# The second angle table of a one-core SSM and gated-mix kernel: nine direct slots times w and two chained complex products in place of eight slots and four products

## The chip, the cores and the metric

The kernel runs on one core of a Trainium2 chip. The metric is the device time of one execution in microseconds. The kernel before takes 200.22 us (median of three runs, 199.91 to 201.16). A measured execution is a little longer than the span of its profile, which runs from the first to the last instruction that was recorded.

Five engines work side by side, each through its own queue in order: PE (matrix products), DVE (element-wise work on vectors), ACT (functions, scaling, copies out of PSUM), POOL (fills) and SP (which here only issues transfers). They wait for each other through semaphores.

## The reference, cut to what matters

```
x = u                                    # (1, 2048, 512), bf16
g = sigmoid((x * gate_w).sum(-1))
# a: a long convolution over the 2048 positions, for each of 512 channels d
dt    = exp(log_dt)                                   # (512, 1)
logdA = dt * (A_re + 1j*A_im)                         # (512, 128)
P     = exp(logdA[:, :, None] * l)                    # l = arange(2048), rounded to bf16
K     = einsum("dn,dnl,dn->dl", C, P, dt * B).real    # (512, 2048)
a     = irfft(rfft(u, padded) * rfft(K, padded)) + u * Dskip
# b: the two positions with the largest x @ w_r go through a gated FFN, and are added to x
b     = x + scatter(y_selected * sigmoid(r_selected))
out   = g * a + (1 - g) * b
```

The lag l is rounded to bf16, so above 256 only every second, fourth or eighth lag is distinct. Every distinct lag is the sum of a first part t1 (multiples of 8, up to 248, 32 of them) and a second part t2 (21 of them, in the list T2). So the kernel needs exp(logdA * t1) and w * exp(logdA * t2) as two tables per channel, with w = C * dt * B, and forms K for all pairs by matrix products over the 128 states n.

## The kernel before, in words

Channels go in two halves h = 0, 1 of 256. The states n lie on the 128 partitions. The work of a half is this chain:

- `exps1`, `exps2` (L533, L536) on ACT: real exponentials (magnitudes) of the table slots, one ACTIVATE of 128x512 for each slot, for both halves at once. Those of `exps2` for half 1 go to `ST` and are parked in DRAM (`park`, L880), since their place in SBUF is needed in between. L897 brings them back into `EB[1]` and `BS[1]`.
- `trig` (L541): for four angles at a time, four scaled angles (`SCL`, L404, on ACT or DVE), a sine (ACT), a scalar step on DVE that adds a quarter turn (L554), and the second sine, which is the cosine. The angle and sine buffers (`ARG`, `SNC`) are two, used in turn.
- `tab1(h)` (L559): the first table, 32 values of t1, products of magnitudes with sines and cosines on DVE.
- `tab2(h)` (L585): the second table `TQ[h]`, 21 slots, imaginary and real part. Slots 0 to 7 (t2 = 0..7) are made directly and multiplied by w. Eight factors for steps of 256 are made in `BS`. Slots 8 to 20 are four complex products (`far`, L609) of earlier slots with such factors. A complex product (`cmul`, L569) is six DVE operations: four products into scratch `QA` and two sums.
- `kgen(h)` (L748): 128 table products on PE (L756), copied out into `KA[h]`; then the selection matmuls (L769, L772, L775), which pick and regroup the columns of `KA` into `KC`. Its slots are grouped by four in the order of T2.
- `kspec(h)` (L779): the spectrum of K by matmuls with constants `KP` (L791), loaded at L896 over the place of the first table of half 0, so once `kgen(0)` is done.
- `products(h)` (L797): spectrum of u times spectrum of K on DVE, most of it in operations of 128x2048.
- `inverse(h)` (L830): inverse transform on PE (L845), scaled by the gate, added, and written out.

Beside it run `routing` (gate, selection of two positions and the FFN), `forward` (the transform of u in two blocks, L736 and L738: a group is eight matmuls, in the second block with a ninth) and `xupd` (L868, the update of x on PE, L873 and L874, and ACT).

Buffers share places. `TQ[1]` lies over `KA[0]`, so `tab2(1)` may write only after the selection of half 0 has read it; its real part also lies over `NG`, constants of `forward`. `EB[1]` lies over `TQ[0]`, so the parked magnitudes come back after the table products of half 0.

Nobody writes the order of the engines' queues by hand. `Prog.op` (L67) collects operations with the buffers and keys that they read and write; `Prog.schedule` (L107) puts them into one queue per engine, by a planned start, and among equal ones by the longest planned path to the end plus a priority (`boost`, `prio`). Operations of the helpers `EV` (copies out of PSUM, L400) and `SCL` go to ACT or DVE, whichever the plan has free earlier. So an edit of one function moves instructions on all engines. The helpers' lines in the profile are L387 (`TT`, product or sum of two tensors on DVE), L391/L392 (`TS`, scalar step on DVE), L394 (`STT`), L398 (`AC`, ACT), L402 (`EV`), L406 (`SCL`) and L409 (a transfer). A DVE operation that reads or writes a key of an earlier DVE operation waits for that one's semaphore.

## Time and profile before

| | us |
|---|---|
| median of three runs | 200.22 |
| the profiled execution | 200.09 |
| its span | 198.3 |
| DVE busy in the span | 170.9 (86%), 281 instructions |
| PE busy | 162.3 (82%), 1490 matmuls |
| ACT busy | 140.8 (71%), 232 instructions |
| POOL busy | 3.4 (2%) |
| mean granted PE clock | 0.944 of full speed |

Times in the profile count from the start of the span. A timeline row has the start, the length, engine, line, operation, the shapes of output and input, and how many instructions were merged; in brackets, how long the engine was idle ahead of it and what ended that. A row of a window has the length of the window and for each engine the busy time and number of instructions, then the granted PE clock, the busy share of the transfer engines and GB/s. A row of a group has the busy time, the mean length of one in ns, and the idle time ahead. [...]

### The profile page before, as it was taken

Reading aid. Unit: us, or ns where it says so; the run is one execution under the profiler, and the core shown is the slowest. Engines: PE = TensorE matmul, PEld = TensorE weight load, DVE = VectorE, ACT = ScalarE, POOL = GpSimd, SP = SyncE. Lnnn points to the kernel's source line nnn. Section 1 sums busy time; section 2 is a strip of 40 time slices with the busy share of each in tenths; the row PEclk is TensorE's granted clock in tenths of the full one; section 3 lists DMA queues with packets and bytes.
Section 4 is the critical chain, followed back from the end, with each engine's and each line's share of the span. In section 5 each row is a group of like instructions: output and inputs, shape, how many; then the busy total and the mean of one; then the engine's idle time right before and its main releaser. Section 6 shows DMA issues by size and latency. Waiting matters only on the chain.

```text
span 198.3 us, 3623 instructions
## 1 busy us (share of the span) xinstructions
PE 162.3 (82%) x1490; PEld 106.5 (54%) x1490; DVE 170.9 (86%) x281; ACT 140.8 (71%) x232; POOL 3.4 (2%) x7
## 2 busy tenths in 40 slices
PE   0074599999999999999996499950988999999791
PEld 0063434774344444455753038740866888888680
DVE  0659635599999999999768999999999999999983
ACT  3669999979999999879999984640663553642500
POOL 6000000000000000000000000000000000000000
PEclk9999759999999999999999759996699999999998
DMA  5999999309320220200089400000029000012333
GB/s 92 281 259 370 293 410 406 95 8 338 82 53 3 53 53 0 53 3 0 3 304 451 198 2 3 0 0 0 3 46 377 3 0 3 0 46 71 98 106 106
DMA packets 22097, 23.17 MB, mean 117 GB/s; under 512 B 13121, under 2 KB 19394, under 8 KB 21442
## 3 DMA queue, kind: packets, MB, share of 16 engines
q1 hardware_dynamic: 20738, 22.63, 35.5%
q10 hardware_dynamic: 1344, 0.33, 1.4%
q8 instruction: 11, 0.18, 0.3%
q14 instruction: 4, 0.03, 0.0%
HBM read 19.02 MB, written 3.15 MB: 112 GB/s over the span
## 4 chain that ended last, share of the span: by engine, by line
PE 61%; DVE 19%; ACT 11%; DMA 4%; SPq 1%; issue 1%; DVEq 0%
PE ps L736 29%; DVE AR L387 17%; PE ps L791 7%; ACT AR L398 5%; ACT AR L402 5%; PE ps L845 5%; PE ps L756 5%; DMA AR<-in_A_u_dram 4%; PE ps L769 3%; PE ps L738 2%; PE ps L873 2%; PE ps L711 2%; DVE AR L394 2%; PE ps L625 1%; PE ps L874 1%; PE ps L700 1%
## 5 line engine op out<-in xcount | busy, mean ns | idle before, releaser
L387 DVE TENSOR_TENSOR AR<-AR 128x1024 bf16<-128x1024 bf16 (+7 forms) x184 | 135.4, 796 | 7.8 <-DMA AR<-in_A_A_re_dram 6.3
L402 ACT ACTIVATE AR<-ps 128x1024 bf16<-128x1024 f32 (+4 forms) x56 | 44.0, 810 | 27.8 <-PE ps L791 14.0
L398 ACT ACTIVATE AR<-AR 128x512 bf16<-128x512 f32 (+4 forms) x84 | 59.5, 773 | 5.2 <-DVE AR L391 2.5
L736 PE MATMUL ps<-AR 128*128 128x512 bf16 x256 | 61.3, 391 | 0.0
L736 PEld LDWEIGHTS ps<-AR 128*128 128x128 bf16 x256 | 25.3, 100 | 30.7 <-issue 3.4
L845 PE MATMUL ps<-AR 128*128 128x256 bf16 x256 | 28.7, 273 | 1.1 <-DVE AR L387 1.1
L398 ACT ACTIVATE AR<-ps,AR 128x256 bf16<-128x256 f32 (+1 forms) x40 | 20.3, 564 | 10.1 <-PE ps L845 5.4
L791 PE MATMUL ps<-AR 128*128 128x256 bf16 x224 | 26.0, 274 | 1.7 <-ACT AR L402 1.7
L845 PEld LDWEIGHTS ps<-AR 128*128 128x128 bf16 x256 | 24.9, 98 | 4.5 <-DVE AR L387 1.6
L791 PEld LDWEIGHTS ps<-AR 128*128 128x128 bf16 x224 | 21.7, 99 | 6.1 <-ACT AR L402 3.1
L406 ACT ACTIVATE AR<-AR 128x256 int32<-128x256 f32 (+1 forms) x50 | 21.1, 483 | 0.1
L756 PE MATMUL ps<-AR 128*128 128x84 bf16 x256 | 13.4, 213 | 8.0 <-DVE AR L387 7.6
L756 PEld LDWEIGHTS ps<-AR 128*128 128x128 bf16 x256 | 11.9, 105 | 11.2 <-DVE AR L387 7.9
L625 PE MATMUL ps<-AR 128*128 128x128 bf16 x64 | 6.0, 270 | 12.8 <-DMA AR<-in_A_u_dram 11.3
L391 DVE TENSOR_SCALAR AR<-AR 128x1024 int32<-128x1024 int32 (+4 forms) x24 | 13.2, 551 | 0.3
L625 PEld LDWEIGHTS ps<-AR 128*128 128x128 bf16 x64 | 5.1, 124 | 13.5 <-DMA AR<-in_A_u_dram 11.3
L873 PE MATMUL ps<-AR 128*128 128x512 bf16 x16 | 7.3, 455 | 4.5 <-ACT AR L398 4.5
L402 DVE CAST AR<-ps 128x1024 bf16<-128x1024 f32 (+1 forms) x7 | 8.0, 1140 | 3.2 <-PE ps L736 1.7
L874 PE MATMUL ps<-AR 128*128 128x512 bf16 x16 | 7.4, 465 | 0.0
L406 DVE TENSOR_SCALAR AR<-AR 128x256 int32<-128x256 f32 (+1 forms) x22 | 5.6, 296 | 1.9 <-ACT AR L398 1.8
L402 DVE COPY AR<-ps 128x1024 bf16<-128x1024 bf16 (+1 forms) x7 | 4.7, 684 | 2.9 <-PE ps L625 2.6
L769 PE MATMUL ps<-AR 128*32 128x128 bf16 (+1 forms) x96 | 6.4, 383 | 0.5 <-ACT AR L402 0.5
(36 smaller groups left out, 56.6 us busy)
## 6 DMA issues: line engine op xcount, KB each, us to landing
AR<-c_ksp SPq DMA_DIRECT2D x1, 3584.0 KB, 13.5
AR<-in_A_u_dram SPq DMA_DIRECT2D x2, 1024.0 KB, 8.9
AR<-c_fwd SPq DMA_DIRECT2D x1, 2048.0 KB, 8.0
AR<-c_fwdn SPq DMA_DIRECT2D x8, 256.0 KB, 4.2
AR<-c_inv SPq DMA_DIRECT2D x1, 2048.0 KB, 7.7
out_dram<-AR SPq DMA_DIRECT2D x16, 128.0 KB, 2.2
AR<-in_B_w_gate_dram SPq DMA_DIRECT2D x1, 1792.0 KB, 11.0
AR<-in_B_w_up_dram SPq DMA_DIRECT2D x2, 896.0 KB, 11.4
```

The costliest lines, as they stand in the source:

```text
L387: return P.op(DVE, lambda h: h.tensor_tensor(out=o, in0=a, in1=b, op=op), rd, wr, cost=tt_cost(o, a, b), **k)
L391: return P.op(DVE, lambda h: h.tensor_scalar(out=o, in0=a, scalar1=s1, scalar2=None, op0=op0), rd, wr, cost=c, **k)
L398: return P.op(ACT, lambda h: h.activation(out=o, in_=a, func=func, scale=scale, bias=bias), rd, wr, cost=0.185 + nel(o) * 0.833e-3 + (0.09 ...
L402: return P.op((ACT, DVE), (lambda h: h.activation(out=o, in_=a, func=ACTF.Copy), lambda h: h.tensor_copy(o, a)), rd, wr, cost=(0.185 + n * ...
L406: return P.op((ACT, DVE), (lambda h: h.activation(out=o, in_=a, func=ACTF.Copy, scale=c), lambda h: h.tensor_scalar(out=o, in0=a, scalar1= ...
L625: last = h.transpose(bb(0, 128, db * 256 + t_ * 128, (1, 128)), U(0, 128, (2 * q + t_) * D + db * 128, (1, 128)), IDN(0, (1, 128)))
L736: last = h.matmul(o, w, U(0, 128, (blk * 8 + st * 2 + par) * D, (1, D)), start=(par + st == 0), stop=(par * 4 + st == 7 and blk == 0))
L756: last = hh.matmul(pb(0, 128, (g - b0) * 84, (1, 84)), TP[h][1 - part](0, 128, g * 128, (1, 128)), TQ[h][1 - part](0, 128, g * 84, (1, 84) ...
L769: last = hh.matmul(pb(32 * g, 32, c4, (256, njg), (4, 64)), lw, KA[h](0, 128, c4 + 4 * (8 * bk + g), (16, njg), (84, 64)), start=True, sto ...
L791: last = hh.matmul(pb(0, 128, n * 256, (1, 256)), KP(0, 128, u * 2048 + tau * 128, (1, 128)), KC[h](0, 128, jg * 256, (1, 256)), start=(k ...
L845: last = hh.matmul(pb(0, 128, e * 256, (1, 256)), G(0, 128, ((par * 2 + part) * 4 + ft) * 512 + (2 * t2 + e) * 128, (1, 128)), X(0, 128, h ...
L873: h.matmul(pb(0, 128, c0, (1, D)), IDN(0, (1, 128)), U(0, 128, tb * D, (1, D)), start=True, stop=False)
```

## The change

`MAG2` has nine magnitudes to compute in place of sixteen; that of lag 0 is filled with ones by POOL. T2 has the same 21 values in another order. Angles per half are 11 (four, four and three) in place of 16. Nine slots of the table (t2 = 0, 1, 2, 3, 258, 256, 512, 768, 1024) are made directly in `TQ` and multiplied by w in one complex product of 2304 elements per operation. Two further complex products fill the rest from these: slots 13 to 20 are slots 0 to 7 times the factor of t2 = 4 (2048 elements), and slots 9 to 12 are slots 5 to 8 times the factor of t2 = 1024 (1024 elements); the two factors are in `BN`. `cmul` writes two of its four products straight to the output and adds in place. The selection in `kgen` reads its columns by the new grouping `T2BASE`. The park in DRAM has 2560 columns in place of 4096, and its load is written ahead of that of the spectrum constants, with a high priority.

```diff
...
@@ -256,10 +256,12 @@
 BLK, NBLK, HF, HC = 1024, 2, 2, 256
 T1 = [8 * k for k in range(16)] + [8 * (31 - k) for k in range(16)]
 ANG1 = [124 - 8 * s for s in range(16)]
-T2 = list(range(8)) + [256, 258, 260, 262, 512, 516, 768, 772, 1024, 1280, 1536, 1792, 2048]
+T2 = [0, 1, 2, 3, 258, 256, 512, 768, 4, 5, 6, 7, 262, 260, 516, 772, 1024, 1280, 1536, 1792, 2048]
+T2BASE = [(0, 4), (13, 17), (8,)]
 NJ = len(T2)
-ANG2 = [124 + b for b in range(8)] + [256 * a for a in range(1, 9)]
-MAG2 = list(range(8)) + [256 * a for a in range(1, 9)]
+ANG2 = [124 + t for t in T2[:8]] + [1148, 1024, 4]
+MAG2 = [None] + T2[1:8] + [1024, 4]
+NM = len(MAG2)
...
@@ -435,13 +437,12 @@
    ...
-        BS = [(B("bsi%d" % i, o, 4 * KB), B("bsr%d" % i, o + 4 * KB, 4 * KB)) for i, o in enumerate((oG, oE))]
-        EB = [B("eb%d" % i, o, 4 * KB) for i, o in enumerate((oG, oE))]
-        ST = B("st", oE, 8 * KB)
-        B_st = [lambda p0, n, c, *d, k=k: ST(p0, n, c + 2 * KB * k, *d) for k in range(2)]
+        EB = [B("eb%d" % i, o, NM * 512) for i, o in enumerate((oG, oE))]
+        ST = B("st", oE, NM * 512)
         PK = Buf(P, "park", AR[:, :], "dram", 0, 4, BF)
-        park = nc.dram_tensor("park", (128, 4 * KB), BF).ap()
-        QA = [B("qa0", oG + 8 * KB, 7680), B("qa1", oE + 8 * KB, 7680)]
+        park = nc.dram_tensor("park", (128, NM * 256), BF).ap()
+        QA = [B("qa%d" % i, o + NM * 512, 9 * KB) for i, o in enumerate((oG, oE))]
+        BN = [(B("bni%d" % i, o + 14 * KB, KB), B("bnr%d" % i, o + 15 * KB, KB)) for i, o in enumerate((oG, oE))]
...
@@ -534,21 +535,23 @@
...
         def exps2(ts):
+            for b in (EB[0], ST):
+                P.op(POOL, lambda h, b=b: h.memset(b(0, 128, 0, (4 * NM, 64), (1, 4)), 1.0), [], [(b, ("e", 0))], cost=0.4)
             for i, m in enumerate(MAG2):
-                k = i // 8
-                d = (EB[0], BS[0][1])[k]
-                AC(two(d, B_st[k], (i % 8) * 4, 32), AL(0, 128, 0, (HC, 2), (4, 64), (1, 4)), ACTF.Exp, [AL], [(d, ("e", i % 8)), (ST, i)], scale=float(m), tset=ts)
+                if i:
+                    AC(two(EB[0], ST, i * 4, 4 * NM), AL(0, 128, 0, (HC, 2), (4, 64), (1, 4)), ACTF.Exp, [AL], [(EB[0], ("e", i)), (ST, ("e", i))], scale=float(m), tset=ts)
         def trig(h, angs, ts, neg):
             k = na[0] % 2
             na[0] += 1
             a, ah, s = ARG[k], ARH[k], SNC[k]
             for i, t in enumerate(angs):
                 SCL(a(0, 128, i * HC, (1, HC)), B16(0, 128, h * HC, (1, HC)), float(t), [B16], [(a, i)])
-            ks = [(a, i) for i in range(4)]
-            lo = bass.AP(ah.tensor, ah.offset, [[ah.ap[0][0], 128], [2 * HC, 4], [8, 64], [2, 4]])
-            n = 4 * HC
+            na_ = len(angs)
+            ks = [(a, i) for i in range(na_)]
+            lo = bass.AP(ah.tensor, ah.offset, [[ah.ap[0][0], 128], [2 * HC, na_], [8, 64], [2, 4]])
+            n = na_ * HC
             def so(k):
-                return s(0, 128, k * n, (4, 4), (16, 64), (1, 4))
+                return s(0, 128, k * n, (4, na_), (4 * na_, 64), (1, 4))
             AC(so(0), lo, ACTF.Sin, ks, [(s, "s")], scale=SC16, tset=ts)
             w = a(0, 128, 0, (1, n))
             TS(w, w, 16384.0, ALU.add, ks, ks)
...
-        def cmul(h, outs, a, b, nd, rda, rdb, wr):
-
+        def cmul(h, outs, a, b, rda, rdb, wr):
...
-                return t(0, 128, i * 5 * HC, *d)
-            TT(q(0), a(1), b(1), MUL, rda + rdb, [(t, 0)])
-            TT(q(1), a(0), b(0), MUL, rda + rdb, [(t, 1)])
-            TT(q(2), a(1), b(0), MUL, rda + rdb, [(t, 2)])
-            TT(outs(1), q(0), q(1), SUB, [(t, 0), (t, 1)], wr(1))
-            TT(q(0), a(0), b(1), MUL, rda + rdb, [(t, 0)])
-            TT(outs(0), q(2), q(0), ADD, [(t, 0), (t, 2)], wr(0))
+                return t(0, 128, i * 9 * HC, *d)
+            TT(q(0), a(0), b(0), MUL, rda + rdb, [(t, 0)])
+            TT(q(1), a(1), b(0), MUL, rda + rdb, [(t, 1)])
+            TT(outs(1), a(1), b(1), MUL, rda + rdb, wr(1))
+            TT(outs(0), a(0), b(1), MUL, rda + rdb, wr(0))
+            TT(outs(1), outs(1), q(0), SUB, [(t, 0)], wr(1))
+            TT(outs(0), outs(0), q(1), ADD, [(t, 1)], wr(0))
         def tab2(h, ts):
-            (qi, qr), (bi, br), eb = TQ[h], BS[h], EB[h]
+            (qi, qr), (bi, br), eb = TQ[h], BN[h], EB[h]
             tq = lambda p: (qi, qr)[p]
-            n = 4 * HC
-            for g in range(4):
+            TW = 4 * NJ
+            for g in range(3):
                 s = trig(h, ANG2[4 * g:4 * g + 4], ts[g // 2], False)
-                if g < 2:
-                    im, re = [b_(0, 128, 16 * g, (4 * NJ, 64), (1, 16)) for b_ in (qi, qr)]
-                    src = eb(0, 128, 16 * g, (32, 64), (1, 16))
-                    ek = [(eb, ("e", 4 * g + i)) for i in range(4)]
-                    ki, kr = (qi, ("s", g)), (qr, ("s", g))
-                else:
-                    im, re = [b_(0, 128, 16 * (g - 2), (32, 64), (1, 16)) for b_ in (bi, br)]
-                    src = re
-                    ek = [(br, ("e", 4 * (g - 2) + i)) for i in range(4)]
-                    ki, kr = (bi, ("i", g)), (br, ("r", g))
-                TT(im, src, s(0, 128, 0, (16, 64), (1, 16)), MUL, ek + [(s, "s")], [ki])
-                TT(re, src, s(0, 128, 2 * n, (16, 64), (1, 16)), MUL, ek + [(s, "c")], [kr] + (ek if g > 1 else []))
-                if g < 2:
-                    v = lambda part: tq(part)(0, 128, 16 * g, (4 * NJ, 64), (4, 4), (1, 4))
-                    w = lambda part: WW(0, 128, (1 - part) * D + h * HC, (4, 64), (0, 4), (1, 4))
-                    cmul(h, v, v, w, n, [ki, kr], [WW], lambda p: [(ki, kr)[p]])
-            sk = [(b, ("s", g)) for b in (qi, qr) for g in range(2)]
-            b2, b3 = [(bi, ("i", 2)), (br, ("r", 2))], [(bi, ("i", 3)), (br, ("r", 3))]
-            def far(j, cnt, ss, a0, sa, rdb):
-                cmul(h, lambda p: tq(p)(0, 128, 4 * j, (4 * NJ, 64), (4, cnt), (1, 4)), lambda p: tq(p)(0, 128, 0, (4 * NJ, 64), (4 * ss, cnt), (1, 4)),
-                     lambda p: (bi, br)[p](0, 128, 4 * a0, (32, 64), (4 * sa, cnt), (1, 4)), cnt * HC, sk, rdb, lambda p: [(tq(p), ("f", j))])
-            far(8, 4, 2, 0, 0, b2)
-            far(12, 2, 4, 1, 0, b2)
-            far(14, 2, 4, 2, 0, b2)
-            far(16, 5, 0, 3, 1, b2 + b3)
+                nn = len(ANG2[4 * g:4 * g + 4])
+                for b_, kk, o_s, sk in ((qi, "s", 0, "s"), (qr, "c", 2 * nn * HC, "c")):
+                    if g < 2:
+                        TT(b_(0, 128, 16 * g, (TW, 64), (1, 16)), eb(0, 128, 16 * g, (4 * NM, 64), (1, 16)), s(0, 128, o_s, (16, 64), (1, 16)), MUL,
+                           [(eb, ("e", 4 * g + i)) for i in range(4)] + [(s, sk)], [(b_, ("a", g))])
+                    else:
+                        bb = bi if b_ is qi else br
+                        TT(b_(0, 128, 32, (TW, 64), (1, 4)), eb(0, 128, 32, (4 * NM, 64), (1, 4)), s(0, 128, o_s, (12, 64), (1, 4)), MUL,
+                           [(eb, ("e", 8)), (s, sk)], [(b_, ("a", 2))])
+                        TT(bb(0, 128, 0, (8, 64), (1, 8)), eb(0, 128, 32, (4 * NM, 64), (1, 8)), s(0, 128, o_s + 4, (12, 64), (1, 8)), MUL,
+                           [(eb, ("e", 8)), (eb, ("e", 9)), (s, sk)], [bb])
+            ka = lambda p: [(tq(p), ("a", g)) for g in range(3)]
+            ks = ka(0) + ka(1)
+            sl = lambda p, j, c: tq(p)(0, 128, 4 * j, (TW, 64), (4, c), (1, 4))
+            cmul(h, lambda p: sl(p, 0, 9), lambda p: sl(p, 0, 9), lambda p: WW(0, 128, (1 - p) * D + h * HC, (4, 64), (0, 9), (1, 4)), ks, [WW], ka)
+            bn = lambda p, j, c: (bi, br)[p](0, 128, 4 * j, (8, 64), (0, c), (1, 4))
+            cmul(h, lambda p: sl(p, 13, 8), lambda p: sl(p, 0, 8), lambda p: bn(p, 1, 8), ks, [bi, br], lambda p: [(tq(p), "n")])
+            cmul(h, lambda p: sl(p, 9, 4), lambda p: sl(p, 5, 4), lambda p: bn(p, 0, 4), ks, [bi, br], lambda p: [(tq(p), "f")])
 
 
         def routing():
@@ -762,17 +757,18 @@
                 pb = misc()
                 def sel(hh, bk=bk, pb=pb):
                     last = None
-                    njg = 2 if bk < 2 else 1
+                    base = T2BASE[bk]
+                    njg = len(base)
                     for g in range(4):
                         for c4 in range(4):
                             lw = CB(0, 128, c4, (4, 32))
-                            last = hh.matmul(pb(32 * g, 32, c4, (256, njg), (4, 64)), lw, KA[h](0, 128, c4 + 4 * (8 * bk + g), (16, njg), (84, 64)),
+                            last = hh.matmul(pb(32 * g, 32, c4, (256, njg), (4, 64)), lw, KA[h](0, 128, c4 + 4 * (base[0] + g), (16, njg), (84, 64)),
                                              start=True, stop=(bk + g > 0), tile_position=(0, 32 * g))
                             if bk + g == 0:
                                 last = hh.matmul(pb(0, 32, c4, (4, 64)), CB(0, 128, 0, (1, 32)), DSK(0, 128, h * HC + c4, (4, 64)), start=False, stop=True, tile_position=(0, 0))
...
-                            last = hh.matmul(pb(0, 128, 256 + c4, (4, 64)), CB(0, 128, c4, (4, 128)), KA[h](0, 128, c4 + 80, (84, 64)), start=True, stop=True)
+                            last = hh.matmul(pb(0, 128, 256 + c4, (4, 64)), CB(0, 128, c4, (4, 128)), KA[h](0, 128, c4 + 48, (84, 64)), start=True, stop=True)
...
@@ -877,7 +873,7 @@
 
         exps1(0)
         exps2(0)
-        DMA([(bass.AP(park.tensor, 0, [[4 * KB, 128], [1, 4 * KB]]), ST(0, 128, 0, (1, 4 * KB)))], [ST], [PK], 1048576)
+        DMA([(bass.AP(park.tensor, 0, [[NM * 256, 128], [1, NM * 256]]), ST(0, 128, 0, (1, NM * 256)))], [ST], [PK], 655360)
...
@@ -893,9 +889,8 @@
         P.boost = 60.0
         kgen(0)
         P.boost = 0.0
+        DMA([(EB[1](0, 128, 0, (1, NM * 256)), bass.AP(park.tensor, 0, [[NM * 256, 128], [1, NM * 256]]))], [PK], [(EB[1], ("e", i)) for i in range(NM)], 655360, prio=1e5)
         DMA([(KP(0, 128, 0, (1, 7 * 2048)), kp_c[:, :])], [], [KP], 3670016)
-        DMA([(B("eb1b", oE, 8 * KB)(0, 128, 0, (1, 4 * KB)), bass.AP(park.tensor, 0, [[4 * KB, 128], [1, 4 * KB]]))], [PK],
-            [(EB[1], ("e", i)) for i in range(8)] + [(BS[1][1], ("e", i)) for i in range(8)], 1048576)
         tab2(1, (1, 1))
         kspec(0)
         kgen(1)
```

## The prediction

> **What bounds the kernel now.** I read the windows first, then the chain of work that ended last, then each engine's timeline, then the groups by shape for prices.
>
> ```profile
> core 0: us, PE busy (x) PEld busy (x) DVE busy (x) ACT busy (x) POOL busy (x), PEclk, DMA share, GB/s
> 41.50:88.40 46.90, 46.90 (x317) 22.38 (x316) 46.83 (x81) 43.44 (x67) 0.00 (x0) 1.00 0.25 68
> 88.40:105.50 17.10, 17.10 (x224) 10.96 (x222) 13.22 (x21) 16.70 (x32) 0.00 (x0) 1.00 0.31 119
> 105.50:139.00 33.50, 20.71 (x134) 12.45 (x132) 32.98 (x54) 20.35 (x29) 0.00 (x0) 0.84 0.19 82
> 139.00:191.00 52.00, 48.97 (x526) 42.11 (x527) 51.72 (x62) 25.64 (x46) 0.00 (x0) 0.97 0.20 67
> ```
>
> Until 105.5 us PE has no idle time at all. From 105.5 us on DVE has next to none: 84.70 of 85.50 us. So there are two bounds, one behind the other. The chain agrees:
>
> ```profile
> 78.75 0.21 PE ps L738
> ...
> 80.69 0.22 PE ps L738
> ...
> 95.28 0.22 PE ps L873
> 95.49 0.21 PE ps L874
> ...
> 121.25 17.75 DVE AR L387 x28
> ...
> 170.86 15.87 DVE AR L387 x20
> ...
> 186.77 4.67 PE ps L845 x40
> ```
>
> The hand-over is the start of the second half's angle table, tab2(1), on DVE:
>
> ```profile
> 104.28 0.68 DVE L387 TENSOR_TENSOR AR<-AR 128x1024 bf16<-128x1024 bf16 x1
> 105.54 4.30 DVE L387 TENSOR_TENSOR AR<-AR 128x1024 bf16<-128x1024 bf16 x7 [0.57 <-PE ps L775]
> ...
> 121.25 29.48 DVE L387 TENSOR_TENSOR AR<-AR 128x2048 bf16<-128x2048 bf16 x40 [0.47 <-ACT AR L402]
> ```
>
> tab2(1) overwrites what the selection matmuls of the first half (L769 to L775) read, so it waits for the last of them. I call that moment S, 105.5 us now. **The end is S plus DVE's work behind it**, plus a tail (inverse matmuls, last DVE step, output) that the edit leaves alone.
>
> **Term 1: DVE's work in one table.**
>
> ```profile
> L387 DVE TENSOR_TENSOR AR<-AR 128x2048 bf16<-128x2048 bf16 x48 | 57.2, 1214 | 0.6 <-ACT AR L402 0.5
> L387 DVE TENSOR_TENSOR AR<-AR 128x1024 bf16<-128x1024 bf16 x90 | 56.6, 680 | 0.7 <-PE ps L775 0.6
> L391 DVE TENSOR_SCALAR AR<-AR 128x1024 int32<-128x1024 int32 x16 | 10.9, 679 | 0.0
> L387 DVE TENSOR_TENSOR AR<-AR 128x1280 bf16<-128x1280 bf16 x12 | 9.4, 809 | 0.0
> L387 DVE TENSOR_TENSOR AR<-AR 128x512 bf16<-128x512 bf16 x24 | 9.0, 411 | 0.0
> ```
> ```profile
> 60.71 4.89 DVE L387 TENSOR_TENSOR AR<-AR 128x1024 bf16<-128x1024 bf16 x8
> 65.53 0.68 DVE L391 TENSOR_SCALAR AR<-AR 128x1024 int32<-128x1024 int32 x1
> ```
>
> Eight products of 1024 take 65.53 - 60.71 = 4.82 us, 0.603 each, where one lasts 0.68: neighbours overlap by 0.075. With that taken off, the prices are 0.336 (512), 0.605 (1024), 0.734 (1280) and 1.139 us (2048), a line of 0.07 us plus 0.523 ns per element. On it 2304 elements cost 1.275, 256 cost 0.20, and a 768-wide scalar step 0.47.
>
> Before, per half: 4 scalar steps 2.42, 8 magnitude products 4.84, complex products 18 x 0.605 + 12 x 0.336 + 6 x 0.734 = 19.32; sum 26.6. After: scalar steps 2 x 0.605 + 0.47 = 1.68; magnitude products 4 x 0.605 + 2 x 0.20 + 2 x 0.336 = 3.49; complex products 6 x (1.275 + 1.139 + 0.605) = 18.1; sum 23.3. The complex products handle 32256 elements either way; only their number falls, 36 to 18. **Gain 3.3 us per half.**
>
> Against it stands the order of the new products: in five places one waits for the one just ahead.
>
> ```profile
> 7.91 0.43 DVE L391 TENSOR_SCALAR AR<-AR 128x512 f32<-128x512 f32 x1
> 8.37 0.43 DVE L392 TENSOR_SCALAR AR<-AR 128x512 f32<-128x512 f32 x1
> ```
>
> Such a pair starts 0.46 apart for 0.43 long: no overlap, 0.03 extra, so about 0.11 each, 0.55 per half. [...]
>
> **Term 2: how far S moves.** ACT first: seven of its exponentials go (16 magnitudes become 9).
>
> ```profile
> 20.52 16.22 ACT L398 ACTIVATE AR<-AR 128x512 bf16<-128x512 f32 x31
> ...
> 38.05 2.20 ACT L398 ACTIVATE AR<-AR 128x1 f32<-128x1 bf16 x4
> ```
>
> At 16.22 / 31 = 0.523 us that is 3.7 us, so the first sine (the four operations are two small ones and two sines) ends near 35.6 instead of 39.3. DVE's own queue holds the first scalar step a little longer: the forward eviction at 34.26, then some 1.4 us of routing steps and a sign copy. I put it at 36.8, against 41.51:
>
> ```profile
> 34.26 1.21 DVE L402 CAST AR<-ps 128x1024 bf16<-128x1024 f32 x1
> ...
> 41.51 0.67 DVE L391 TENSOR_SCALAR AR<-AR 128x1024 int32<-128x1024 int32 x1
> ...
> 86.54 4.21 DVE L387 TENSOR_TENSOR AR<-AR 128x1280 bf16<-128x1280 bf16 x4
> ```
>
> From there to the end of tab2(0) (the first of those four, 87.3) was 45.8 us of nearly unbroken work. Now it is 3.3 less, 0.55 more, 0.5 more for other instructions that the new order puts in between, and by my estimate 0.6 more of waits for the expert's matmuls. 36.8 + 44.15 gives 80.95.
>
> PE is where this counts. Its queue before, at the end of the first table product (ps2 at L756 is that product, kgen(0); L736/L738 are forward groups, L873/L874 updates of x, L769 and L772 the selection):
>
> ```order
> L756 MATMUL ps2<-AR 128x84 x8
> L873 MATMUL ps0<-AR 128x512
> L874 MATMUL ps0<-AR 128x512
> L736 MATMUL ps1<-AR 128x512 x8
> L738 MATMUL ps1<-AR 128x512
> L769 MATMUL ps3<-AR 32x128
> ```
>
> and with the change, where L751, L731/L733 and L765/L768 are the product, the groups and the selection:
>
> ```order
> L751 MATMUL ps2<-AR 128x84 x24
> L731 MATMUL ps0<-AR 128x512 x8
> L733 MATMUL ps0<-AR 128x512
> L751 MATMUL ps2<-AR 128x84 x8
> L731 MATMUL ps1<-AR 128x512 x8
> L733 MATMUL ps1<-AR 128x512
> L765 MATMUL ps3<-AR 32x128
> L768 MATMUL ps3<-AR 32x64
> ```
>
> The first table product now stands behind the ninth forward group of the second block (before: the thirteenth), and the selection ahead of the last group and of all updates. The ninth group ends at 80.69 + 0.22 = 80.9: PE arrives when the table is ready, within my error. I take 0.3 us of waiting. What left the queue ahead of the selection is one forward group and five updates of 0.43 us:
>
> ```profile
> 101.38 0.38 PE L738 MATMUL ps<-AR 128*128 128x512 bf16 x1
> ...
> 104.83 0.67 PE L775 MATMUL ps<-AR 128*128 128x64 bf16 x4
> ```
>
> One group is 80.69 - 78.75 = 1.94 by the chain, so S = 105.5 - 1.94 - 2.15 + 0.3 = **101.7**.
>
> The parked magnitudes must be there by then.
>
> ```profile
> 99.37 0.34 SPq L409 DMA_DIRECT2D AR<-park  x1
> 99.76 0.46 SPq L409 DMA_DIRECT2D AR<-c_ksp  x1
> ```
> ```profile
> AR<-c_ksp SPq DMA_DIRECT2D x1, 3584.0 KB, 13.5
> ...
> AR<-park SPq DMA_DIRECT2D x1, 1024.0 KB, 4.8
> ```
>
> They were already issued ahead of the spectrum constants, so **that edit changes nothing by itself**; I give it 0. Both waited for kgen(0), which ends about 4 us earlier; at 640 instead of 1024 KB they land no later than 101, and the constants near 110, 15 us before DVE's first spectrum product.
>
> The rest I put at nothing. The two memsets that fill the magnitude of lag 0 run on POOL, beside ACT's exponentials:
>
> ```profile
> L499 POOL MEMSET AR<- 128x512 bf16 x1 | 0.5, 524 | 0.0
> ```
>
> Half that size each, they would cost at most 0.5 us were they waited for. Per half, five scaled angles fewer and two of eight sines fewer relieve ACT and DVE ahead of the table; that relief is inside the 36.8 and the waits below. The regrouped selection has the same matmuls, the constants the same size.
>
> **Term 3: DVE behind S.** DVE's queue before, near the end of tab2(1), with the table (512, 1280 and the forms with 64) and the spectrum products (2048, 1024) mixed:
>
> ```order
> L387 TENSOR_TENSOR AR<-AR 128x512
> L387 TENSOR_TENSOR AR<-AR 128x1280
> L387 TENSOR_TENSOR AR<-AR 128x64x8
> L387 TENSOR_TENSOR AR<-AR 128x2048
> L387 TENSOR_TENSOR AR<-AR 128x1280 x2
> L387 TENSOR_TENSOR AR<-AR 128x64x20
> L387 TENSOR_TENSOR AR<-AR 128x1024
> ```
>
> and now, the table's complex products in a row and the spectrum products behind them (the last two rows):
>
> ```order
> L389 TENSOR_TENSOR AR<-AR 128x2304 x2
> L389 TENSOR_TENSOR AR<-AR 128x64x36 x4
> L389 TENSOR_TENSOR AR<-AR 128x2048 x2
> L389 TENSOR_TENSOR AR<-AR 128x64x32 x4
> L389 TENSOR_TENSOR AR<-AR 128x64x16 x2
> L389 TENSOR_TENSOR AR<-AR 128x1024 x2
> L389 TENSOR_TENSOR AR<-AR 128x64x16 x2
> L389 TENSOR_TENSOR AR<-AR 128x2048 x6
> L389 TENSOR_TENSOR AR<-AR 128x1024 x2
> ```
>
> From S the table needs 4 x 0.605 + 0.47 + 1.07 + 18.1 = 22.1, plus 0.55. New waits lie in its first 6 us: the third sine may only overwrite its buffer once the first product has read it, the real products need the last forward group off PE, and the third cosine comes behind that group's eviction on ACT.
>
> ```profile
> L398 ACT ACTIVATE AR<-AR 128x1024 bf16<-128x1024 int16 x32 | 33.0, 1052 | 2.6 <-DVE AR L391 2.5
> ```
>
> Bounds: 0 if the products already queued cover them, 2.6 if two sines of 1.05 and a scalar step stand bare; products cover about half, I take 1.2. Behind it wait all of DVE and kgen(1). The table ends at 125.5. Before, at 138.9, DVE had finished table plus eight spectrum products (six of 2048, two of 1024: 8.0 us); now it stands there at 133.7. PE's idle time in this stretch (33.50 less 20.71 us) shrinks too, but PE was not the bound there. **Gain 5.2 us.** The first half's DVE saving is mostly spent waiting: after tab2(0) at 81 DVE has the 13.2 us that it did between 88.4 and 105.5, is ready for tab2(1) near 95, and stands until S.
>
> The profiled execution took 200.09 us around a span of 198.3, 0.13 below the median of 200.22. 200.09 - 5.2 = **194.9 us**.
>
> **Rivals.** *The table comes late and PE waits (17%).* PE's queue is in order, with six forward groups behind kgen(0). ACT is 93% busy between 41.5 and 88.4 (43.44 of 46.90) and feeds every table step; if DVE waits on it, tab2(0) ends later, and each us past 80.9 moves S by one. Three us late gives 197.9; 5.2 late, at 86.1, takes the whole gain: 200.1. Against it: ACT loses exponentials and sines too. A long wait costs twice:
>
> ```profile
> 112.00:118.00 6.00, 4.94 (x12) 1.23 (x13) 5.98 (x11) 5.28 (x9) 0.00 (x0) 0.50 0.00 0
> ...
> 139.00:142.00 3.00, 2.95 (x43) 2.91 (x44) 3.00 (x3) 1.36 (x3) 0.00 (x0) 0.51 0.00 0
> ```
>
> after stretches with PE idle it was granted half its clock for 3 to 6 us. [...]
>
> *The long products fall off the fast rate (7%).*
>
> ```profile
> L387 DVE TENSOR_TENSOR AR<-AR 128x1024 f32<-128x1024 bf16 x2 | 2.4, 1214 | 0.0
> ```
>
> A slow form costs 1.21 us per 1024. If rows of 36 elements, updated in place, ran so, each of six would cost 1.2 us more: 7.2 in tab2(0), on PE's wait, and 7.2 in tab2(1). That is about 209; it is slower than before from 0.43 us extra per instruction. Against it: today's forms with runs of 4 and repeated operands all hold 0.68.
>
> *No new waits (16%).* S at 101.4 and nothing of 1.2 or 0.55: 7.2 us gained, 192.9.
>
> **How the numbers follow.** The forecast has 60%, 193.5 to 196.5 around it. The range, 192.6 to 198.8, reaches to the third rival and to a table nearly 4 us late. One per cent, about what a measurement of this kernel can tell from no change, is 2 us: below 198.2 lie the forecast, the third rival and half of the first (0.81); within, 0.11; slower, the second rival and the first at its worst, 0.08.
>
> **What would show it.** Right: the first table product on PE near 81 with under 1 us of idle; DVE idle before S, S near 101.7; a 2304-wide product at 1.35 us; PE's idle ahead of kgen(1) gone. Wrong: more than 3 us of PE waiting for DVE near 81, DVE waiting on ACT by more than 2 us behind S, or spectrum products waiting for kspec(0).

## The result and the profile after

The changed kernel takes **194.0 us** (median of 4 runs, 193.47 to 194.25) beside 200.06 us for the kernel before on the same chip (4 runs, 199.56 to 201.16). The ratio is 0.9686, with a 95% interval of 0.964 to 0.9732. The forecast was 194.9. The profiled execution took 193.47 us around a span of 191.7.

The windows, cut near the places that correspond to those of before (the first table, up to S, the second table, the rest up to 7.3 us ahead of the end of the span); busy time with the number of instructions for PE, its weight loads, DVE, ACT and POOL, then granted clock, DMA share and GB/s:

```profile
37.00:81.00 44.00, 44.00 (x368) 22.40 (x365) 43.41 (x62) 38.12 (x62) 0.00 (x0) 1.00 0.27 73
81.00:101.50 20.50, 20.50 (x221) 12.23 (x220) 13.60 (x19) 17.63 (x31) 0.00 (x0) 1.00 0.29 106
101.50:126.00 24.50, 21.48 (x162) 13.29 (x161) 23.36 (x28) 17.87 (x26) 0.00 (x0) 1.00 0.21 90
126.00:184.40 58.40, 49.63 (x514) 41.25 (x512) 57.99 (x69) 26.29 (x47) 0.00 (x0) 0.97 0.18 60
```

The shape is that of before: PE has no idle time from 37 to 101.5 us, and DVE has little behind that (busy for 81.35 of 82.90 us). Two things changed. The stretch from S to the end of the second table is shorter, and PE keeps its full clock in it. In the chain of work that ended last, DVE takes over at 104.8 as it did at 121 before, and the last inverse matmuls take 4.67 us as before:

```profile
104.83 3.17 DVE AR L389 x4
...
180.15 4.67 PE ps L841 x40
```

DVE's timeline at the start of the first table, at its end, and around S:

```profile
35.80 0.69 DVE L393 TENSOR_SCALAR AR<-AR 128x1024 int32<-128x1024 int32 x1
...
78.37 2.42 DVE L389 TENSOR_TENSOR AR<-AR 128x1024 bf16<-128x1024 bf16 x3
...
95.39 0.68 DVE L393 TENSOR_SCALAR AR<-AR 128x1024 int32<-128x1024 int32 x1
100.23 1.29 DVE L389 TENSOR_TENSOR AR<-AR 128x1024 bf16<-128x1024 bf16 x2 [4.15 <-PE ps L771]
102.17 0.56 DVE L393 TENSOR_SCALAR AR<-AR 128x768 int32<-128x768 int32 x1 [0.65 <-ACT AR L400]
...
104.83 35.56 DVE L389 TENSOR_TENSOR AR<-AR 128x256 bf16<-128x256 bf16 x36 [0.35 <-ACT AR L400]
```

The first scalar step begins at 35.80 (41.51 before). Of the three products from 78.37 the first two belong to tab2(0) and the third (2048 wide, 1.22 us) does not, so the table is ready at 79.6. DVE then has work until 96, stands 4.15 us, and starts tab2(1) at S = 100.23 (105.54 before). Behind S it waits twice for ACT, 0.65 and 0.35 us, and then not again until the tail: the waits that the prediction priced at 1.2 us sum to 1.0.

A row further on gives the end of the second table:

```profile
123.30 10.21 DVE L389 TENSOR_TENSOR AR<-AR 128x1024 bf16<-128x1024 bf16 x10
```

The first of these ten is the table's last product, so the table ends 0.60 later, at 123.90. The tenth, a 2048-wide product of 1.22 us, begins at 133.51 - 1.22 = 132.29, and the eight between are the spectrum products that stood ahead of 138.92 before. At this point the kernel is 6.63 us ahead, and nothing is gained or lost after it: 59.4 us remain to the end of the span in both.

PE around the first table product and at the second:

```profile
79.61 0.38 PE L733 MATMUL ps<-AR 128*128 128x512 bf16 x1
79.83 1.07 PE L751 MATMUL ps<-AR 128*128 128x84 bf16 x24
...
99.54 0.66 PE L771 MATMUL ps<-AR 128*128 128x64 bf16 x4
```
```profile
120.91 3.23 PE L787 MATMUL ps<-AR 128*128 128x256 bf16 x28 [0.24 <-ACT AR L404]
124.04 1.07 PE L751 MATMUL ps<-AR 128*128 128x84 bf16 x24
```

kgen(0) follows the ninth group without a gap, 0.2 us after the table was ready: PE and DVE meet there almost exactly. At kgen(1) PE had stood 7.60 us before; now it does not wait, and the half clock that followed (0.51 from 136 to 142 before) is 1.00.

In the groups by shape, the new one (count, busy time, mean ns of one):

```profile
L389 DVE TENSOR_TENSOR AR<-AR 128x2304 bf16<-128x2304 bf16 x12 | 15.9, 1350 | 0.1
```

The new 2304-wide products last 1.350 us, the 1.35 of the forecast's line.

One difference comes ahead of everything that the edit moves in PE's queue: up to 38 us PE runs the same matmuls in the same order in both. TensorE's granted clock near the start, before first and after second:

```profile
24.00:28.00 4.00, 4.00 (x11) 1.58 (x10) 1.15 (x6) 4.00 (x9) 0.00 (x0) 0.50 1.02 401
28.00:31.00 3.00, 3.00 (x13) 1.34 (x12) 1.57 (x8) 3.00 (x7) 0.00 (x0) 0.78 1.03 410
```
```profile
24.00:28.00 4.00, 4.00 (x13) 1.55 (x12) 1.42 (x7) 4.00 (x9) 0.00 (x0) 0.60 1.01 403
28.00:31.00 3.00, 3.00 (x16) 1.49 (x15) 2.40 (x9) 3.00 (x7) 0.00 (x0) 1.00 1.02 407
```

PE is busy throughout in both, and gets 4 x 0.50 + 3 x 0.78 = 4.34 us of full-rate work before, 5.40 after: 1.06 us more. So the 5.31 us by which S came earlier are 1.94 for one group and 2.15 for five updates, as predicted, about 1.06 of clock, and 0.16 left over.

### The profile page after: what moved, and what is told of

It reads as the page before. It is cut to its first block, busy times and chain, and to the rows that moved or that the text cites. A ratio compares the mean times of both kernels' runs of the same rounds, so it can differ in the third digit from the quotient of the medians.

```text
span 191.7 us, 3562 instructions
## 1 busy us (share of the span) xinstructions
PE 160.6 (84%) x1490; PEld 105.7 (55%) x1490; DVE 163.5 (85%) x240; ACT 130.4 (68%) x214; POOL 3.9 (2%) x9
## 4 chain that ended last, share of the span: by engine, by line
PE 46%; DVE 40%; ACT 4%; DMA 4%; issue 2%; SPq 1%; DVEq 0%
DVE AR L389 38%; PE ps L731 30%; DMA AR<-in_A_u_dram 4%; PE ps L751 3%; PE ps L841 2%; ACT AR L400 2%; ACT AR L404 2%; PE ps L733 2%; PE ps L706 2%; DVE AR L396 2%; PE ps L765 2%; PE ps L620 1%; PE ps L695 1%; SPq L484 1%; PE ps L632 1%
## 5 line engine op out<-in xcount | busy, mean ns | idle before, releaser
L389 DVE TENSOR_TENSOR AR<-AR 128x1024 bf16<-128x1024 bf16 (+7 forms) x148 | 130.4, 939 | 11.4 <-DMA AR<-in_A_A_re_dram 6.2
L404 ACT ACTIVATE AR<-ps 128x1024 bf16<-128x1024 f32 (+5 forms) x58 | 45.2, 818 | 27.0 <-PE ps L787 14.5
L731 PE MATMUL ps<-AR 128*128 128x512 bf16 x256 | 60.5, 387 | 0.0
L400 ACT ACTIVATE AR<-AR 128x512 bf16<-128x512 f32 (+4 forms) x73 | 50.5, 757 | 3.4 <-DVE AR L389 2.2
L731 PEld LDWEIGHTS ps<-AR 128*128 128x128 bf16 x256 | 24.8, 99 | 28.9 <-issue 2.3
L841 PE MATMUL ps<-AR 128*128 128x256 bf16 x256 | 30.9, 281 | 6.0 <-DVE AR L389 4.4
L841 PEld LDWEIGHTS ps<-AR 128*128 128x128 bf16 x256 | 25.3, 101 | 11.1 <-DVE AR L389 5.8
L400 ACT ACTIVATE AR<-ps,AR 128x256 bf16<-128x256 f32 (+1 forms) x40 | 19.9, 566 | 15.6 <-PE ps L841 10.2
L787 PE MATMUL ps<-AR 128*128 128x256 bf16 x224 | 26.2, 273 | 2.5 <-ACT AR L404 2.5
L787 PEld LDWEIGHTS ps<-AR 128*128 128x128 bf16 x224 | 21.3, 98 | 7.2 <-ACT AR L404 4.6
L408 ACT ACTIVATE AR<-AR 128x256 int32<-128x256 f32 (+1 forms) x41 | 17.2, 488 | 0.0
L393 DVE TENSOR_SCALAR AR<-AR 128x1024 int32<-128x1024 int32 (+5 forms) x22 | 11.5, 529 | 1.8 <-ACT AR L400 1.5
L620 PEld LDWEIGHTS ps<-AR 128*128 128x128 bf16 x64 | 5.7, 133 | 12.7 <-DMA AR<-in_A_u_dram 11.0
L751 PE MATMUL ps<-AR 128*128 128x84 bf16 x256 | 11.7, 200 | 1.1 <-ACT AR L404 1.1
L751 PEld LDWEIGHTS ps<-AR 128*128 128x128 bf16 x256 | 10.8, 97 | 3.1 <-ACT AR L404 1.5
L869 PE MATMUL ps<-AR 128*128 128x512 bf16 x16 | 6.2, 386 | 1.7 <-ACT AR L400 1.4
L404 DVE CAST AR<-ps 128x1024 bf16<-128x1024 f32 (+1 forms) x6 | 6.8, 1125 | 0.5 <-PE ps L733 0.5
L733 PE MATMUL ps<-AR 128*128 128x512 bf16 x16 | 6.1, 379 | 0.0
```

What stands on the lines that cost most here:

```text
L389: return P.op(DVE, lambda h: h.tensor_tensor(out=o, in0=a, in1=b, op=op), rd, wr, cost=tt_cost(o, a, b), **k)
L393: return P.op(DVE, lambda h: h.tensor_scalar(out=o, in0=a, scalar1=s1, scalar2=None, op0=op0), rd, wr, cost=c, **k)
L400: return P.op(ACT, lambda h: h.activation(out=o, in_=a, func=func, scale=scale, bias=bias), rd, wr, cost=0.185 + nel(o) * 0.833e-3 + (0.09 ...
L404: return P.op((ACT, DVE), (lambda h: h.activation(out=o, in_=a, func=ACTF.Copy), lambda h: h.tensor_copy(o, a)), rd, wr, cost=(0.185 + n * ...
L408: return P.op((ACT, DVE), (lambda h: h.activation(out=o, in_=a, func=ACTF.Copy, scale=c), lambda h: h.tensor_scalar(out=o, in0=a, scalar1= ...
L620: last = h.transpose(bb(0, 128, db * 256 + t_ * 128, (1, 128)), U(0, 128, (2 * q + t_) * D + db * 128, (1, 128)), IDN(0, (1, 128)))
```

## The experiments

The planner's order is that of the changed kernel unless a text says otherwise. "Products" are tensor_tensor products of 1024 elements; S is read from each profile. Medians come from 4 to 10 runs of each.

### Is S hung on the first table? Extra products behind tab2(0)

Six products are put into DVE's order behind the last of tab2(0), and kgen(0) is made to wait for them.

```
+ at = last operation of tab2(0) in DVE's order
+ for i in range(6):
+     QA[0] part i % 2 = sl(0, 4) * sl(0, 4)   (scratch), placed behind at, on which kgen(0) depends
```

> After with six more 128x1024 products on DVE at the end of tab2(0); they write scratch, so the output is unchanged, and kgen(0) waits for them. Theory (S hangs on the first table): the table is ready 3.7 us later, near 83.2 us, PE stands idle some 3.3 us ahead of kgen(0), S goes from 100.2 to 103.5 and the time from 194.0 to 197.3 us. Rival (DVE has 4.15 us of idle time ahead of S, which takes up the six products): the time stays at 194.0.

Then three and twelve of them, after the first result:

> After with three extra products at the end of tab2(0). Theory as for twelve: PE idles about 1.6 us, too short for the clock to fall, S is 1.6 us later and all executions lie at 195.4 to 196.2 us. Rival: some executions near 198 to 200.

> After with twelve extra products at the end of tab2(0) (six gave either 196.0 or about 200.0 us, with mean granted clocks of 0.979 and about 0.945). Theory (a PE idle time of more than about 3.5 us is followed by a stretch at half clock; six products left 3.46, on the border): PE idles some 7 us ahead of kgen(0), its granted clock then falls to 0.50 for some 6 us, S is 7.1 us later for the products and about 3 to 4 more for the clock, near 110.5, and all executions lie near 204 to 205 us. Rival (the 200.0 us have another cause): the clock stays at 1.00, S is about 107.3 and the time about 201 us.

PE at kgen(0) and DVE at S, for three, six and twelve:

```profile
81.06 1.08 PE L751 MATMUL ps<-AR 128*128 128x84 bf16 x24 [1.64 <-DVE AR L940]
...
101.47 1.29 DVE L389 TENSOR_TENSOR AR<-AR 128x1024 bf16<-128x1024 bf16 x2 [4.15 <-PE ps L771]
```
```profile
82.36 1.07 PE L751 MATMUL ps<-AR 128*128 128x84 bf16 x24 [3.46 <-DVE AR L940]
...
102.76 1.29 DVE L389 TENSOR_TENSOR AR<-AR 128x1024 bf16<-128x1024 bf16 x2 [4.14 <-PE ps L771]
```
```profile
86.79 1.86 PE L751 MATMUL ps<-AR 128*128 128x84 bf16 x24 [7.05 <-DVE AR L940]
...
109.62 1.29 DVE L389 TENSOR_TENSOR AR<-AR 128x1024 bf16<-128x1024 bf16 x2 [4.14 <-PE ps L771]
```

Three products: 194.88 us (194.72 to 195.68), beside 193.51 for the changed kernel measured with it on one chip. That is 1.4 more for 1.64 us of PE idle time, a little under the expected 195.4 to 196.2. Twelve: 203.1 us (202.37 to 203.84), 9.6 more. So what is late at tab2(0) comes out at the end. DVE's 4.15 us of idle time ahead of S are still there each time: it waits for PE, and extra work on DVE does not fill that wait when PE waits for the work. The rival that this idle time absorbs it falls.

Six products gave two levels: the profiled execution 196.01 us at a mean granted clock of 0.979, the three others 199.94 to 200.51 us at 0.940 to 0.948. The expected 197.3 fits neither. In the profiled one S came 2.53 us later than in the changed kernel's first profile (102.76 for 100.23) and the end 2.54 later (196.01 for 193.47), so in it the end follows S. The twelve show what a longer wait does. Their windows:

```profile
83.00:86.00 3.00, 0.00 (x0) 0.00 (x0) 3.00 (x6) 0.00 (x0) 0.00 (x0) 0.84 0.00 0
86.00:88.00 2.00, 1.21 (x18) 1.21 (x19) 2.00 (x4) 0.15 (x1) 0.00 (x0) 0.50 0.00 0
...
90.00:92.00 2.00, 2.00 (x6) 0.70 (x5) 2.00 (x3) 1.17 (x2) 0.00 (x0) 0.54 0.00 0
92.00:94.00 2.00, 2.00 (x31) 1.39 (x29) 1.97 (x4) 1.27 (x4) 0.00 (x0) 1.00 0.04 8
```

The clock column reads 0.84 over 83 to 86, so it fell to 0.50 at about 85.0; 0.54 over 90 to 92 puts its return at 91.8. PE had stopped at 79.7. The drop came some 5 us into the idle time, lasted 6.8 us, and 5 us of it fell on work: about 2.5 us lost on PE. S against the changed kernel's second profile (100.55) is 9.07 later, 7.05 for the idle time and 2.0 more. The expected 3 to 4 was too much, because the drop began while PE still stood; the kind of effect, the second price of a long wait, was right. With 1.64 us of idle time the clock stayed at 1.00; with 3.46 it stayed there in the one profile that exists. That the three slower executions with six products lost their 4 us to such drops fits their clocks, but no trace of them shows it.

What length of wait brings a drop stays open. The clock held at 1.00 through the 3.46 us with six products, in the one profile, and fell within the 7.05 us with twelve. But it also fell behind a wait of only 2.67 us in the run with the exponentials given back (below), and of the two half-clock rows that the prediction shows, the first follows gaps of at most 2.09 us, and the stretch of the second begins within the 7.60 us of idle time ahead of kgen(1). The border of about 3.5 us in what was expected of twelve products was the author's estimate from the two levels with six; no run shows such a border.

### Does DVE set the end behind S?

The same six products behind tab2(1).

> After with the same six products at the end of tab2(1) instead. Theory (DVE sets the pace behind S): S stays at 100.2, the table ends 3.7 us later and the time is 197.7 us. Rival (PE with its updates, kgen(1) and inverse matmuls sets the end behind S): 194.0, with DVE's extra work hidden.

```profile
124.25 3.70 DVE L940 TENSOR_TENSOR AR<-AR 128x1024 bf16<-128x1024 bf16 x6
127.87 13.02 DVE L389 TENSOR_TENSOR AR<-AR 128x2048 bf16<-128x2048 bf16 x12
```

Median 197.83 us (196.5 to 198.42), ratio to before 0.9855 (0.9784 to 0.9926). S is at 100.45 in its profile, close to the 100.23 expected to stay. 3.6 us of products cost 3.8 us. The rival, PE as the bound behind S, falls.

### Is it the exponentials? Given back to the new kernel, taken from the old one

```
+ olds = the first 7 exponentials of the second table on ACT
+ for q in olds: the same activation again, behind the last of them; whoever reads q waits for it
```

> After with seven of its exponentials done a second time on ACT, behind the others, in an otherwise unchanged order: this takes back the 3.7 us by which ACT was relieved. Theory (the first sine, and with it the whole first table, starts earlier only because ACT is free earlier): DVE's first scalar step goes from 35.8 to about 39, PE waits about 3 us at kgen(0), S is about 103.2 and the time 196.5 to 197.5 us. Rival (ACT catches up before kgen(0), the table is bound by DVE and the order): 194.0 to 194.6.

```profile
38.97 0.69 DVE L393 TENSOR_SCALAR AR<-AR 128x1024 int32<-128x1024 int32 x1
```
```profile
42.35 1.58 PE L695 MATMUL ps<-AR 128*128 128x2 bf16 x56 [2.67 <-ACT AR L404]
...
83.45 1.06 PE L751 MATMUL ps<-AR 128*128 128x84 bf16 x24
```
```profile
43.45:46.84 3.39, 3.06 (x31) 1.85 (x29) 3.25 (x6) 3.37 (x6) 0.00 (x0) 0.50 0.44 129
```

196.85 us (196.38 to 197.59), ratio 0.9816 (0.9765 to 0.9866): the number as expected, 2.85 us more than 194.0. The place was not. PE did not wait at kgen(0), which has no idle time in front of it; it lost the time at 42, ahead of the expert's first matmuls (L695). Their input waits for an eviction on ACT that now stands behind the exponentials, and PE starts nothing else in the 2.67 us ahead of them. The loss is not that wait alone: behind it the clock stood at 0.50 for 3.4 us, with PE busy for most of them. In the profiles PE is 2.19 us later than in the changed kernel at L695 (42.35 for 40.16) and 3.62 later at kgen(0) (83.45 for 79.83); about 1.4 us are added in that stretch.

The kernel before without seven of its exponentials:

```
+ POOL fills seven magnitudes with ones
  for i, m in enumerate(MAG2):
+     if i > 8: one element instead of 512 x 128, same place in ACT's order
```

> The kernel before with seven of the sixteen exponentials of its second table shrunk to one element each (POOL fills their magnitudes with ones; these values are left out of the computation), in an unchanged order: ACT's relief alone. Theory (in the order of before kgen(0) stands behind the thirteenth group, where PE arrives at 88.5 when the table is ready at 87.3): the table is ready some 3 us earlier, PE takes no notice, S stays at 105.5 and the time at 200.0 us. Rival (the gain comes from ACT's relief): about 197.

```profile
41.46 1.06 ACT L398 ACTIVATE AR<-AR 128x1024 bf16<-128x1024 int16 x1 [3.97 <-DVE AR L391]
```
```profile
38.87 1.28 DVE L402 COPY AR<-ps 2x1024 bf16<-2x1024 bf16 x2 [0.37 <-PE ps L693]
...
40.75 0.67 DVE L391 TENSOR_SCALAR AR<-AR 128x1024 int32<-128x1024 int32 x1
...
104.77 1.90 DVE L387 TENSOR_TENSOR AR<-AR 128x1024 bf16<-128x1024 bf16 x3 [0.57 <-PE ps L781]
```

200.42 us (199.38 to 201.73, 10 runs), ratio 1.0024 (0.998 to 1.0068): no gain. ACT was free earlier and stood 3.97 us idle, because DVE's first scalar step moved by only 0.76 (40.75 for 41.51), no more than S (104.77 for 105.54), that is by the clock of this execution. In the order of before it stands behind copies that wait for PE. So the relief is worth nothing in the old order and 2.85 us in the new one, a clock drop included. The expectation had the right time for a partly wrong reason: the table did not come 3 us earlier either.

### Is S where PE's queue puts it?

One forward group and two updates are moved ahead of the selection of the first half.

```
+ late = [o for o in PE_order behind sels[0] if o in forward groups or o in xupd[:2]]
+ PE_order: late moved ahead of sels[0]
```

> After with one change in PE's order: the last forward group and two of the updates stand ahead of the selection of the first half, as in the kernel before, where one more group and five updates did. Theory (S is where PE's queue puts it): S goes from 100.2 to about 103.0 (1.94 for the group, 0.86 for two updates), the wait for the real part's forward group behind S, 0.3, goes away, and the time is about 196.5 us. Rival (PE does the same work in either order and DVE makes up for it behind S): 194.0.

```profile
79.07 1.07 PE L751 MATMUL ps<-AR 128*128 128x84 bf16 x24
...
101.59 0.66 PE L771 MATMUL ps<-AR 128*128 128x64 bf16 x4
```
```profile
102.28 1.29 DVE L389 TENSOR_TENSOR AR<-AR 128x1024 bf16<-128x1024 bf16 x2 [6.96 <-PE ps L771]
104.22 0.56 DVE L393 TENSOR_SCALAR AR<-AR 128x768 int32<-128x768 int32 x1 [0.64 <-ACT AR L400]
...
106.83 29.82 DVE L389 TENSOR_TENSOR AR<-AR 128x256 bf16<-128x256 bf16 x30 [0.31 <-ACT AR L400]
```

196.11 us (195.48 to 197.44), ratio 0.9784 (0.9726 to 0.9842). From kgen(0) to S it is 23.21 us, 2.81 more than in the changed kernel (20.40): the 2.80 of the moved work. DVE stands 6.96 us instead of 4.15, again 2.81. On the clock of the execution S is 2.05 later (102.28 for 100.23), because kgen(0) itself began 0.76 earlier in this profile, and the time rises by 2.1. The rival falls. The waits behind S stayed (0.64 and 0.31), so they are waits for ACT's own queue and not for the forward group; that part of the expectation was wrong.

### The order of the two loads

```
- SP: park -> magnitudes; c_ksp -> spectrum constants
+ SP: c_ksp -> spectrum constants; park -> magnitudes
```

> After with the two transfers on SP swapped: the spectrum constants are issued ahead of the load of the parked magnitudes. Theory (both wait for kgen(0) and share the DMA engines, so the magnitudes land last, some 14 to 15 us behind the issue near 94.9): the first magnitude products of tab2(1) start near 109.5 instead of 100.2 and the time is about 203 us. Rival (the small load gets its share of the engines and lands near 101 anyway): 194.0 to 195.

```profile
94.94 0.34 SPq L411 DMA_DIRECT2D AR<-c_ksp  x1
95.32 1.63 SPq L411 DMA_DIRECT2D AR<-park  x1
```
```profile
108.05 1.29 DVE L389 TENSOR_TENSOR AR<-AR 128x1024 bf16<-128x1024 bf16 x2 [11.58 <-DMA AR<-park]
```

200.7 us (200.19 to 201.67, 10 runs), ratio 1.0032 (0.9998 to 1.0067). The small load lands 12.6 us after its issue instead of 5.0, DVE stands 11.58 us, and the time rises by 6.7, less than the 9 expected, because the load lands at 107.9 and not at 109.5. So the order of the loads is worth nearly the whole gain, but it is not part of the gain: before already issued them this way.

### Finer dependences, and a version that is faster than both

A complex product's two imaginary-only products no longer wait for the real part, and the planner makes its order from that. Part 0 is the imaginary one; the two products that read part 1 wait only for it likewise. (The third group's cosine also gets a second key, since it overlaps another buffer's.)

```
-            TT(q(0), a(0), b(0), MUL, rda + rdb, [(t, 0)])
...
-            TT(outs(0), a(0), b(1), MUL, rda + rdb, wr(0))
+            TT(q(0), a(0), b(0), MUL, rda(0) + rdb, [(t, 0)])
...
+            TT(outs(0), a(0), b(1), MUL, rda(0) + rdb, wr(0))
```

> After with finer dependences in the complex products: the two products that read only the imaginary part need not wait for the real part, so DVE has work behind S while ACT makes the third sine and cosine. The order follows from it; one group more and no more updates move behind the selection. Expected: the 1.0 us of waits behind S shrink to under 0.4 and the time is 193.0 to 193.6 us. Rival (the waits only move to the next product, or the forward group that PE now does later holds back the real part): 194.0 to 195.

> The same, with the updates of x on PE held behind the last forward group. Expected: the forward groups that the real part and their evictions on ACT need come off PE earlier than with the updates among them, and the time is 192.4 to 193.4 us. Rival (the updates hold up DVE's or ACT's later work): 194 or more.

The second adds, for every update, a dependence on the last forward group. DVE of the first, then of the second:

```profile
99.21 1.29 DVE L389 TENSOR_TENSOR AR<-AR 128x1024 bf16<-128x1024 bf16 x2 [3.70 <-PE ps L771]
101.15 0.56 DVE L393 TENSOR_SCALAR AR<-AR 128x768 int32<-128x768 int32 x1 [0.64 <-ACT AR L400]
```
```profile
100.44 1.29 DVE L389 TENSOR_TENSOR AR<-AR 128x1024 bf16<-128x1024 bf16 x2 [5.34 <-PE ps L771]
102.04 0.56 DVE L393 TENSOR_SCALAR AR<-AR 128x768 int32<-128x768 int32 x1 [0.31 <-ACT AR L400]
```

192.94 us (191.67 to 193.25), ratio 0.9618 (0.9569 to 0.9667), and 193.1 us (192.31 to 193.43), ratio 0.9632 (0.9586 to 0.9677). Both are about 1 us below the changed kernel, with intervals that overlap its own. In the first the wait of 0.35 is gone and the 0.64 is not, so the waits did not shrink to under 0.4 as expected; S came 1.0 us earlier than in the changed kernel (99.21 for 100.23). In the second only 0.31 is left, but the planner put a forward group inside the selection and S came later. So that group was moved out, behind the selection:

```
+ late = [o for o in forward groups if it stands between the first and the last sel of half 0]
+ PE_order: late moved behind the last of these sels
```

> The kernel with finer dependences and late updates, with the forward group that PE did inside the selection of the first half moved behind it. Theory (S sets the end and DVE now has imaginary products to do meanwhile): S goes from 100.4 to about 99.0 (1.94 less for the group, some 0.5 back for a bank that ACT has to empty), no new wait behind S, and the time from 193.1 to about 191.6 us. Rival (the real part then waits for that group's matmuls and evictions): 193.0 or more.

> The changed kernel once more, beside the others on one chip: 193.5 to 194.5 us, and in its profile a half-clock stretch of 6 to 7 us near the start whose end lies anywhere from 25.5 to 29.2 us, as in all profiles so far; S moves with it by up to 1 us.

```profile
97.97 1.29 DVE L389 TENSOR_TENSOR AR<-AR 128x1024 bf16<-128x1024 bf16 x2 [3.31 <-PE ps L772]
99.58 0.56 DVE L393 TENSOR_SCALAR AR<-AR 128x768 int32<-128x768 int32 x1 [0.31 <-ACT AR L400]
101.86 38.13 DVE L389 TENSOR_TENSOR AR<-AR 128x1024 bf16<-128x1024 bf16 x42 [1.72 <-PE ps L733]
```

**191.83 us** (191.01 to 192.31, 6 runs), ratio 0.9591 (0.955 to 0.9632), beside 193.51 (192.82 to 194.24, 6 runs) and 0.9679 (0.9637 to 0.972) for the changed kernel measured with it on one chip. It is the fastest of all that ran, 1.7 us below the changed kernel, with intervals that just do not overlap. S went from 100.44 to 97.97, and here the wait for the forward group does appear, 1.72 us: theory and rival are both partly right, and by medians, taken on two chips, 1.3 us remain of the 2.5 by which S moved.

## Why the prediction was right

**Term 1, DVE's work in a table: right.** From S to the table's end it forecast 22.1 + 0.55 + 1.2 = 23.85 us; the profile shows 123.90 - 100.23 = 23.67. Two of its prices can be read directly, and both held. The 2304-wide product lasts 1.350. For the in-order waits there is a row of six products in the second table, five of them 2304 wide and the last 2048 wide (1.23):

```profile
106.64 8.06 DVE L389 TENSOR_TENSOR AR<-AR 128x2304 bf16<-128x2304 bf16 x6
```

Five take 6.83 us; at 1.275 each without a wait they would take 6.38, and in four of these five places a product waits for the one just ahead, so each such wait cost 0.114, where 0.11 was put.

**Term 2, S: the mechanism right, the size short.** PE reached kgen(0) when the table was ready, without idle time, and the selection stands one group and five updates earlier. The run that put one group and two updates back moved S, counted from kgen(0), by 2.81 us, where their length is 2.80. But the step "S = 105.5 - 1.94 - 2.15 + 0.3 = 101.7" is the one that was mis-sized: it measured 100.23. 0.3 is the wait that did not come, and about 1.1 is the clock that PE got back earlier in the profiled execution, which the sum had taken over from the profile of before. First scalar step (35.80 for 36.8) and table (79.6 for 80.95) were early by the same amount.

**Its reason for the earlier table was half of the cause.** The step began with ACT's seven exponentials. Without them the old order gains nothing. With them back the new order loses 2.85 us, part of it to a clock drop, and still stands 3.7 us below the kernel before (196.85 beside 200.57). So the relief pays only together with the order, while the new kernel keeps more than half of its gain without it; and where the relief is missing, the time is lost at the expert's matmuls and not at kgen(0).

**Term 3, behind S: right.** From S to the eight products' end it is 33.38 us before and 32.06 after, 1.3 less, where the forecast's own numbers (105.5 to 138.9, 101.7 to 133.7) give 1.4. The waits were 1.0 for 1.2, all of it behind ACT; the forward group that it named as one of them cost nothing here. The forecast that the first half's saving would be spent waiting shows in DVE's idle time between the end of tab2(0) and S: 3.9 us before (18.24 less 14.33 busy), 6.9 after (20.63 less 13.73). PE's idle time ahead of kgen(1) went as foretold.

**The edit at nothing: right.** The loads stand in the same order as before, and DVE never waited for the spectrum constants.

**Sums and readings.** 125.5 and 8.0 make 133.5 and not the 133.7 that stands there, by which the gain would have been 5.4; and the chances of what lies below 198.2 add up to 0.845 and not 0.81. That PE has no idle time until 105.5 holds from 24 us on.

**The rivals.** The late table missed by little: ready at 79.6, asked for at 79.8. The runs with extra products are that rival made real: 1.4 us for 1.64 of waiting, 9.6 for 7.05, the surplus from the clock. The long products stayed at the fast rate, 1.350 us for 2304 elements. "No new waits" was wrong by the 1.0 us behind S and four in-order gaps.

By profile the gain is 6.6 us, by medians 6.06, against 5.2. Without the 1.1 of clock, 5.5 of the 6.6 remain. Whether the early half clock ends sooner in the new order as a rule stays open: it ended near 29.3 and 28.6 us in the two profiles with the old order, and between 25.8 and 28.4 in the twelve with the new one.

## What to carry to other kernels

When the bound passes from one in-order engine to another, find the instruction at which it passes, and count what stands ahead of it in the first engine's queue: here one group and five updates were 4.1 of some 6 us, and of 3.3 us saved on the other engine ahead of that point some 3.0 turned into idle time. Work taken off an engine pays only where the order lets the next engine start sooner, so try the relief and the order separately before naming one as the cause. And keep the place where the two engines meet clear by a margin: a wait there can cost a clock drop besides, as the 7.05 us with twelve products did: the time rose by 9.6.

## What the runs showed of the hardware that was not expected

- TensorE's half-clock stretch near the start lies at a different place in each profile: 22.5 to 29.3 us in that of before, 20.4 to 27.2 after. It lasted 6.8 us in thirteen of the fourteen profiles, and 10.2 us, from 17.1 on, in that of the version with late updates. Later ones lasted 6.8 us before (111.2 to 118.0 and 135.1 to 141.9) and with twelve products (85.0 to 91.8), and 3.4 us after (170.5 to 173.9) and with the exponentials given back (43.4 to 46.8).
- With twelve products, in a wait of 7.05 us without matmuls, the clock fell only about 5.3 us into the idle time and came back 6.8 us later, so the part of the drop that fell on the wait cost nothing.
- With the exponentials given back the clock fell to 0.50 for 3.4 us behind a wait of only 2.67 us.
- With six products the same kernel took 196.0 us in the profiled execution, with 3.46 us of idle time, and about 200.0 in the three others.
- Two loads issued 0.4 us apart on one queue landed in the order of issue in both orders tried: 640 KB took 5.0 us ahead of 3584 KB, and 12.6 us behind them.
